# Sliding-window attention and a channel mix: the first loads ordered by hand

## The chip, the cores and the metric

The kernel runs on one core of a Trainium2 chip. The core has five engines: TensorE (PE, matrix products and transposes), VectorE (DVE), ScalarE (ACT), GpSimd (POOL) and SyncE (SP, which here only issues transfers), and 16 DMA engines that move data between the chip's memory (HBM) and the core's SBUF. Each engine works through its own instructions in order and waits on semaphores for what others make. The metric is the device time of one execution in microseconds (us); lower is better.

## What is computed

The first part is attention over 8 batches of 8 heads, with 576 positions of 64 elements. Each position sees itself and the 127 before it, and a bias falls off linearly with the distance (its slope differs from head to head). The second part mixes each position with the one before it, in two ways, and runs a gated two-layer network of width 512 to 1024 to 512.

```python
scores = scale * q @ k.T                         # B, H, S, D = 8, 8, 576, 64
bias   = -slope[h] * abs(i - j)
attn   = softmax(where(0 <= i - j < 128, scores + bias, -1e9))
x      = (attn @ v).transpose(0, 2, 1, 3).reshape(B, S, 512)
x_prev = x shifted by one position
xk     = mu_k * x + (1 - mu_k) * x_prev
xr     = mu_r * x + (1 - mu_r) * x_prev
out    = sigmoid(xr @ w_r) * (relu(xk @ w_k) ** 2 @ w_v)
```

Inputs and output are float32. The matrix products run in bfloat16.

## The kernel before

One iteration `it` of the kernel is one pair of heads `g` of one batch `b` (4 pairs, 8 batches, so 32 iterations). Its q, k and v land in a ring of four float32 slots, `ldr` for q and k and `vdr` for v. They are cast to bfloat16, q and k are transposed on PE, then come scores, exp, attention times v (AV), normalization and the transpose back:

```python
NBUF = 4
ldr = cst.tile([128, 2, NBUF, 2, NF * D], FP32, name="ldr")
vdr = cst.tile([128, NBUF, 2, NF, D], FP32, name="vdr")

def load_qk(it, npair=1, part=None): ...   # SyncE: q, k of 512 positions into slot it % 4
def load_v(it, j0=0, j1=NF): ...           # SyncE: v, one transfer for each head
def load_tail(b): ...                      # SyncE: the last 64 positions of all heads: tq (q, k), tv (v)
def cast_qk(it, part=None, fq=pool_cast, fk=vec_cast): ...   # ldr -> cs
def cast_v(it, j0=0, j1=NF): ...           # POOL: vdr -> vs_buf[it % 4]
def transp(it): ...                        # PE: cs -> tp, ACT: tp -> qk_buf[it % 4]
def scores(it, pieces, m0): ...            # PE: sa, ACT: exp -> at; DVE: times mask
def av(it, t0, t1): ...                    # PE: sa, DVE: rc, xu (normalized)
def outT(it, t0, t1): ...                  # PE: xu -> tp, ACT: xt, DVE: dl, xk, xr
```

For the first two batches (`it < NEARLY`, 8) the bias and the window are added by extra matmuls (`sid` with `dist`) instead of a mask product. Meanwhile the mask of the later batches is made (`make_mask` on ACT, `copy_mask` on DVE).

The network's work lies in a list of units, each with the PE time that it is reckoned at in ns. `run_units(n)` takes units off the list until their sum comes to n:

```python
def add_units(P, c0, c1):
    for fo in range(NFO):                                   # xk @ w_k, relu on ACT, square on DVE
        units.append(((c1 - c0) * 1.69, lambda fo=fo: mm1(P, c0, c1, fo)))
    for c in range(c0 // 128, c1 // 128):
        units.append((864, lambda c=c: mm3(P, c)))          # xr @ w_r, tanh on ACT
        units.append((864, lambda c=c: mm2(P, c0, c, 0)))   # kk @ w_v, first half
        units.append((864, lambda c=c: mm2(P, c0, c, 1)))   # second half, ot on DVE, store
```

The start: batch 0 is worked on in two ranges of positions (0 to 255, then the rest), so that PE has something to do before all of it has landed. The weights come by transfers that GpSimd issues and that cast from float32 on the way.

```python
load_qk(0, 1, 0)
load_v(0, 0, 2)
load_qk(1, 3, 0)
for g in range(1, G):
    load_v(g, 0, 2)
make_identity(nc, ident)
make_dist()
load_qk(0, 4, 1)
load_tail(0)
for g in range(G):
    load_v(g, 2, NF)
# ... first range of batch 0; at its third step (g == 2):
load_w(wk_sb, moe_w_k)
load_w(wr_sb, moe_w_r)
# ... second range of batch 0, between units of positions 0 to 255:
for g in range(-1, G + 1):
    # ... scores, casts, transposes; load_w(wv_sb, moe_w_v) at g == 0
    if 0 <= g < G:
        av(g, 2, NJ)
        load_qk(G + g)
        load_v(G + g)
        if g == 0:
            load_tail(1)
    # ...
```

In the first range all five engines follow the order of the program. From the second range on, only PE, SyncE and GpSimd do; for ACT and DVE the compiler's scheduler chooses.

From batch 1 on, one loop:

```python
for it in range(G, NIT + 2):
    b, g = divmod(it, G)
    load_qk(it + 4)
    load_v(it + 4)
    if g == 0:
        load_tail(b + 1)
    scores_full(it)
    # bud: what is left over a reserve of 5000, spread over the batch
    run_units(bud * .15)
    # ... transp_tail, units
    if it > G:
        av(it - 1, 0, NJ)
    run_units(bud * .25)
    transp(it + 2)
    cast_qk(it + 3)
    cast_v(it + 3)
    # ... cast_tail, units, masks
    if it > G:
        outT(it - 1, 0, NJ)
        # ... at g == 0: add_units of the batch that is complete
    run_units(bud * .25)
```

PSUM is shared out as two double banks for scores and AV (`p_sa`), one bank for transposes (`p_tp`) and three for the network (`p_mm`).

Of the kernel before, what the change touches and what calls it, by code (L numbers as in the profile page):

```python
# [9 lines left out]
FP32 = mybir.dt.float32  # L10
# [7 lines left out]
def kernel(  # L18
# [56 lines left out]
    xt_buf = [cst.tile([128, NPO, 2 + S], BF16, name=f"xt{i}") for i in range(2)]  # L75


    def load_tail(b):
        if b >= B:
            return  # L80
        tq = tlp.tile([128, H, D], FP32, tag="tq", name="tq")
        tv = tlp.tile([64, H, D], FP32, tag="tv", name="tv")
        T["tl", b] = (tq, tv)
        for src, dst in ((q, tq[0:64]), (k, tq[64:128]), (v, tv)):
            nc.sync.dma_start(out=dst, in_=src[b, :, SM:S, :].rearrange("h p d -> p h d"))

    def load_qk(it, npair=1, part=None):
        if not 0 <= it < NIT:
            return
        b, g = divmod(it, G)  # L90
        s0 = it % NBUF
        for i, src in enumerate((q, k)):
            hs = src[b, 2 * g:2 * g + 2 * npair]
            dst = ldr[:, i, s0:s0 + npair].rearrange("p s h c -> p (s h) c")
            if part is None:
                nc.sync.dma_start(
                    out=dst,
                    in_=hs[:, 0:SM].rearrange("h (p r) d -> p h (r d)", p=128))
            else:
                nc.sync.dma_start(  # L100
                    out=dst[:, :, 128 * part:128 * part + 128],
                    in_=hs[:, 256 * part:256 * part + 256].rearrange(
                        "h (p r) d -> p h (r d)", p=128))

    def load_v(it, j0=0, j1=NF):
        if not 0 <= it < NIT:
# [18 lines left out]
    def cast_qk(it, part=None, fq=pool_cast, fk=vec_cast):  # L125
        if not 0 <= it < NIT:
            return
        cs = csp.tile([128, 2, NF, 2, D], BF16, tag="cs", name="cs")
        T["cs", it, part] = cs
        r0, r1 = (0, NF) if part is None else (2 * part, 2 * part + 2)  # L130
        for i, f in ((0, fq), (1, fk)):
            f(cs[:, i, 0:r1 - r0].rearrange("p r h d -> p h r d"),
              ldr[:, i, it % NBUF].rearrange(
                  "p h (r d) -> p h r d", d=D)[:, :, r0:r1])
# [10 lines left out]
    def cast_tail(b):  # L145
        if b >= B:
            return
        tq, tv = T.pop(("tl", b))
        ts = csp.tile([128, H, D], BF16, tag="ts", name="ts", bufs=2)
        T["ts", b] = ts  # L150
        pool_cast(ts, tq)
        tvb = tv_buf[b % 2]
        if b < 2:
            nc.gpsimd.memset(tvb[:, :, D], 1.0)
            nc.gpsimd.memset(tvb[64:128], 0.0)
            nc.gpsimd.memset(tt_buf[b][:, :, 1], 0.0)
        pool_cast(tvb[0:64, :, 0:D], tv)


    def transp_tail(b):  # L160
        if b >= B:
            return
        ts = T.pop(("ts", b))
        tp = p_tp.tile([128, 1024], BF16, tag="tp", name="tp")
        for g in range(G):
            nc.tensor.transpose(
                tp[:, 128 * g:128 * g + 128],
                ts[:, 2 * g:2 * g + 2].rearrange("p h d -> p (h d)"), ident)
        t4 = tp[:, 0:128 * G].rearrange("p (g t c) -> p g t c", g=G, t=2)
        nc.vector.tensor_copy(out=tt_buf[b % 2][:, :, 2], in_=t4[:, :, 0])  # L170
        nc.vector.tensor_copy(out=tt_buf[b % 2][:, :, 0], in_=t4[:, :, 1])  # L171
# [30 lines left out]
    def scores(it, pieces, m0):  # L202
# [28 lines left out]
        if not early:  # L231
            nc.vector.tensor_tensor(
                out=ah, in0=ah, in1=mask[:, 2 * g:2 * g + 2, m0:m0 + w], op=ALU.mult)

    def scores_full(it):
        scores(it, ((0, 0, 256), (1, 128, 256)), 0)
        scores(it, ((2, 256, 256), (3, 384, 128), (3, 512, 64), (4, 512, 64)), 256)

    def av(it, t0, t1):
        if not 0 <= it < NIT:  # L240
# [23 lines left out]
    def outT(it, t0, t1):  # L264
# [1 line left out]
            return  # L266
        b, g = divmod(it, G)
        xu = T.pop(("xu", it, t0))
        tp = p_tp.tile([128, 1024], BF16, tag="tp", name="tp")
        for t in range(t0, t1):  # L270
            nc.tensor.transpose(  # L271
                tp[:, 128 * t:128 * t + 128],
# [39 lines left out]
    def mm3(P, c):  # L312
        xr = T["xr", P]
        pr = p_mm.tile([128, 512], FP32, tag="mm", name="pr")
        for po in range(NPO):
            nc.tensor.matmul(  # L316
                pr, lhsT=xr[:, po, 128 * c:128 * c + 128], rhs=wr_sb[:, po],
                start=(po == 0), stop=(po == NPO - 1))
        rs = otp.tile([128, DM], BF16, tag="rs", name="rs")
        T["rs", P, c] = rs  # L320
        nc.scalar.activation(out=rs, in_=pr, func=AF.Tanh, scale=0.5)  # L321

# [19 lines left out]
    ident = cst.tile([128, 128], BF16, name="ident")  # L342
    mask = cst.tile([128, H, 768], BF16, name="mask")
    dist = cst.tile([128, 768], BF16, name="dist")
    dist2 = cst.tile([128, 256], BF16, name="dist2")
    sid = cst.tile([128, H, 128], BF16, name="sid")
    MSEG = ((256, 256), (512, 192), (704, 64))
    wk_sb = cst.tile([128, NPO, DF], BF16, name="wk_sb")
# [22 lines left out]

    def make_mask(heads):
        for h in heads:
            nc.scalar.activation(out=mask[:, h, 0:256], in_=dist2,
                                 func=AF.Exp, scale=-(2.0 ** (-(h + 1))))

    def copy_mask():
        for (c0, n) in MSEG:
            nc.vector.tensor_copy(out=mask[:, 0:H, c0:c0 + n], in_=mask[:, 0:H, 0:n])

    def load_w(dst, src):
        nc.gpsimd.dma_start(out=dst, in_=src.rearrange("(i p) w -> p i w", p=128))
# [34 lines left out]
        ENG.PE, ENG.SP, ENG.Pool, ENG.Activation, ENG.DVE})  # L417
    order.__enter__()
    load_qk(0, 1, 0)
    load_v(0, 0, 2)  # L420
    load_qk(1, 3, 0)
    for g in range(1, G):
        load_v(g, 0, 2)
    make_identity(nc, ident)
    make_dist()
    load_qk(0, 4, 1)
    load_tail(0)
    for g in range(G):
        load_v(g, 2, NF)


    make_sid(0)
    make_sid(1)
    cast_qk(0, 0, act_cast, vec_cast)
    transp_part(0, 0)
    cast_qk(1, 0, act_cast, vec_cast)
    cast_v(0, 0, 2)
    load_mu()
    for g in range(G + 2):
        if g < G:  # L440
            scores(g, ((0, 0, 256), (1, 128, 128)), 0)
        if g + 1 < G:
            transp_part(g + 1, 0)
            make_sid(2 * g + 2)
            make_sid(2 * g + 3)
            cast_v(g + 1, 0, 2)
        if g + 2 < G:
            cast_qk(g + 2, 0, act_cast, vec_cast)
        if g == 2:
            load_w(wk_sb, moe_w_k)  # L450
            load_w(wr_sb, moe_w_r)
        if 0 <= g - 1 < G:
            av(g - 1, 0, 2)
        if g == 4:
            cast_qk(0, 1, act_cast, vec_cast)
            transp_part(0, 1)
        if 0 <= g - 2 < G:
            outT(g - 2, 0, 2)
    order.__exit__(None, None, None)
    order = tc.manual_schedule(engines={ENG.PE, ENG.SP, ENG.Pool})  # L460
    order.__enter__()
    add_units(0, 0, 256)

    def second(g, which):
        if not 0 <= g < G:
            return
        if which == 0:
            scores(g, ((1, 256, 128), (2, 256, 256)), 128)
        else:
            scores(g, ((3, 384, 128), (3, 512, 64), (4, 512, 64)), 512)  # L470

    for g in range(-1, G + 1):
        bud = left() / max(1, G - g)
        second(g + 1, 0)
        if g == -1:
            cast_tail(0)
            transp_tail(0)
        run_units(bud * .2)
        second(g + 1, 1)
        if g + 2 < G:  # L480
            cast_qk(g + 2, 1, act_cast, vec_cast)
            transp_part(g + 2, 1)
        if g + 1 < G:
            cast_v(g + 1, 2, NF)
        if g == 0:
            load_w(wv_sb, moe_w_v)
        run_units(bud * .3)
        if 0 <= g < G:
            av(g, 2, NJ)
            load_qk(G + g)  # L490
            load_v(G + g)
            if g == 0:
                load_tail(1)
        run_units(bud * .3)
        if g >= 1:
            outT(g - 1, 2, NJ)
        if g == 2:
            cast_qk(G)
            transp(G)
            cast_v(G)  # L500
        if g == 3:
            cast_tail(1)
            cast_qk(G + 1)
            cast_v(G + 1)
        run_units(bud * .2)
    transp(G + 1)
    transp_tail(1)
    cast_qk(G + 2)
    cast_v(G + 2)
    add_units(0, 256, 512)  # L510

    for it in range(G, NIT + 2):
        b, g = divmod(it, G)
        load_qk(it + 4)
        load_v(it + 4)
        if g == 0:
            load_tail(b + 1)
        scores_full(it)
        if it >= NIT:
            bud = left() if it == NIT else 1 << 30  # L520
        elif g == 0:
            bud = min(left(), 5500.0)
        else:
            bud = max(left() - RESERVE, 0) / (G - g)
# [1 line left out]
        if g == 2:  # L526
            transp_tail(b + 1)
        run_units(bud * .1)
        if it > G:
            av(it - 1, 0, NJ)  # L530
        run_units(bud * .25)
        transp(it + 2)
        cast_qk(it + 3)
        cast_v(it + 3)
        if g == 1:
            cast_tail(b + 1)
        run_units(bud * .25)
        if it == G:
            pool_cast(dist2, dist[:, 0:256])
        if it < NEARLY:  # L540
            make_mask(range(2 * g, 2 * g + 2))
        if it == NEARLY - 1:
            copy_mask()
        if it > G:
            outT(it - 1, 0, NJ)
            if g == 0:
                P, e = divmod(b - 1, 2)
# [4 lines left out]
                    add_units(P, 0, 512)  # L552
        run_units(bud * .25)
    order.__exit__(None, None, None)


# [1 line left out]
_INS = ['q', 'k', 'v', 'moe_mu_k', 'moe_mu_r', 'moe_w_k', 'moe_w_v', 'moe_w_r']  # L558
# [26 lines left out]
```

## Time and profile before

| | |
|---|---|
| median of 3 runs | 291.3 us (288.97 to 294.21) |
| span of the profiled execution | 290.8 us |
| instructions | 6032 |
| read from HBM, written to it | 33.56 MB, 9.44 MB |
| transfers on SyncE's queue, on GpSimd's | 48.4% and 5.6% of 16 engines' span |
| largest groups | pv matmuls (kk with w_v) 73.6 us, kk product on DVE 37.6 us |

How to read it: a row of 40 digits shows how busy an engine was in each fortieth of the span (7.3 us each), 9 for 90% or more. "PEclk" is the clock that was granted to PE, in tenths of its full speed. The chain is followed back from the last instruction: each piece is what the next one waited for. In a list of waits the engine on the left sat idle until the one on the right was done; DMA on the right means a load had not landed. A group is named by the tile that it writes and those that it reads: `ldr<-in_k_dram` is a load of k into the ring, `cs<-ldr` the cast out of it, `tq` and `tv` are the tails. PE's busy time is modelled (matmuls overlap), so it says when PE had work and not how near it was to its peak.

### The profile page before, as it was taken

What the parts mean: (1) busy time and instruction counts of PE and PEld (TensorE: products, weight loads), DVE (VectorE), ACT (ScalarE), POOL (GpSimd) and SP (SyncE); (2) the same over time, 40 slices, a digit from 0 to 9 for tenths busy, and PEclk for the clock granted to TensorE, in tenths of its full rate; (3) what the DMA queues carried; (4) which work ended last, traced back from release to release, by engine and by line L of the source; (5) the groups of instructions that cost most, each with busy time, mean ns of one, the idle gap of its engine ahead of it and who ended that gap; (6) DMA issues with size and microseconds to landing.
All of it is one profiled execution on the core that took longest, in us unless ns stands there. A gap on an engine that the chain in (4) does not pass through costs nothing.

```text
span 290.8 us, 6032 instructions
## 1 busy us (share of the span) xinstructions
PE 248.3 (85%) x2304; PEld 144.1 (50%) x2304; DVE 207.1 (71%) x434; ACT 182.1 (63%) x297; POOL 68.7 (24%) x111
## 2 busy tenths in 40 slices
PE   2859648796769899979999999889899999998994
PEld 1326414454436466545565575545464755544461
DVE  1472315757688898897899797997697978875341
ACT  4654613597758667767676686866695858725350
POOL 5516051405124312421132122321042120000000
PEclk9999977999999999999999999999999999999999
DMA  6997994999109057671564482914851511011021
GB/s 177 230 201 178 180 159 136 275 243 263 28 36 253 17 172 194 202 197 39 163 198 131 159 214 88 291 31 133 245 150 70 149 37 39 0 74 72 36 74 72
DMA packets 73389, 40.77 MB, mean 140 GB/s; under 512 B 48272, under 2 KB 68240, under 8 KB 73360
## 3 DMA queue, kind: packets, MB, share of 16 engines
q1 hardware_dynamic: 71200, 37.76, 48.4%
q0 software_dynamic: 2160, 2.63, 5.6%
q8 instruction: 18, 0.29, 0.4%
q14 instruction: 11, 0.09, 0.1%
HBM read 33.56 MB, written 9.44 MB: 148 GB/s over the span
## 4 chain that ended last, share of the span: by engine, by line
PE 48%; DVE 20%; ACT 15%; DMA 10%; issue 4%; SPq 2%; POOL 0%; DVEq 0%; ACTq 0%; POOLq 0%
PE pv L330 13%; PE pr L316 8%; DMA ldr<-in_k_dram 7%; PE sa L250 4%; DMA tq<-in_k_dram 4%; PE tp L271 4%; DVE kk L307 3%; DVE xk L289 3%; PE tp L179 3%; DVE xu L260 2%; PE sa L227 2%; ACT rs L321 2%; DVE xr L289 2%; DVE ot L336 2%; ACT rl L305 2%
## 5 line engine op out<-in xcount | busy, mean ns | idle before, releaser
L330 PE MATMUL pv<-wv_sb,kk 128*128 128x512 bf16 x288 | 73.6, 386 | 2.7 <-DMA wv_sb<-in_moe_w_v_dram 2.7
L301 PEld LDWEIGHTS <-wk_sb 128*128 128x128 bf16 x416 | 38.9, 100 | 21.3 <-issue 3.9
L307 DVE TENSOR_TENSOR kk<-rl 128x256 bf16<-128x256 bf16 (+2 forms) x104 | 37.6, 381 | 9.5 <-ACT rl L305 8.3
L321 ACT ACTIVATE rs<-pr 128x512 bf16<-128x512 f32 x36 | 21.7, 602 | 27.9 <-PE pr L316 27.8
L330 PEld LDWEIGHTS <-kk 128*128 128x128 bf16 x288 | 25.7, 98 | 27.0 <-issue 3.8
L316 PE MATMUL pr<-wr_sb,xr 128*128 128x512 bf16 x144 | 37.6, 385 | 0.0
L336 DVE SCALAR_TENSOR_TENSOR ot<-rs,pv 128x512 f32<-128x512 bf16 x36 | 24.5, 680 | 10.3 <-PE pv L330 10.3
L120 DVE CAST cs<-ldr 128x512 bf16<-128x512 f32 (+1 forms) x36 | 15.2, 422 | 22.5 <-DMA ldr<-in_k_dram 19.1
L260 DVE TENSOR_TENSOR xu<-sa,rc 128x640 bf16<-128x640 f32 (+2 forms) x36 | 27.0, 749 | 1.1
L271 PE MATMUL tp<-ident,xu 128*128 128x128 bf16 x160 | 15.5, 224 | 12.0 <-DVE xu L260 4.5
L116 POOL TENSOR_SCALAR cs<-ldr 128x512 bf16<-128x512 f32 x28 | 21.4, 766 | 14.0 <-DMA ldr<-in_q_dram 10.4
L271 PEld LDWEIGHTS <-xu 128*128 128x128 bf16 x160 | 11.5, 99 | 22.3 <-DVE xu L260 12.3
L179 PE MATMUL tp<-ident,cs 128*128 128x128 bf16 x224 | 17.1, 219 | 5.3 <-DVE tt_102 L171 2.6
L179 PEld LDWEIGHTS <-cs 128*128 128x128 bf16 x224 | 14.4, 98 | 10.7 <-DVE tt_102 L171 3.4
L230 ACT ACTIVATE at_99<-sa 128x1024 bf16<-128x1024 f32 (+2 forms) x17 | 15.8, 971 | 6.1 <-PE sa L227 6.1
L316 PEld LDWEIGHTS <-xr 128*128 128x128 bf16 x144 | 13.1, 99 | 12.3 <-issue 0.6
L287 DVE TENSOR_TENSOR dl<-xt_106 128x576 bf16<-128x576 bf16 (+2 forms) x20 | 8.8, 442 | 13.1 <-ACT xt_106 L278 13.1
L230 ACT ACTIVATE at_101<-sa 128x1024 bf16<-128x1024 f32 (+2 forms) x17 | 15.8, 974 | 3.5 <-PE sa L227 3.4
L116 POOL TENSOR_SCALAR vs_94<-vdr 128x512 bf16<-128x512 f32 (+1 forms) x9 | 6.4, 708 | 48.0 <-PE sa L250 35.8
L230 ACT ACTIVATE at_98<-sa 128x1024 bf16<-128x1024 f32 (+2 forms) x17 | 15.9, 972 | 2.2 <-PE sa L227 2.2
L287 DVE TENSOR_TENSOR dl<-xt_107 128x576 bf16<-128x576 bf16 x16 | 7.3, 458 | 13.2 <-ACT xt_107 L278 13.2
L278 ACT COPY xt_106<-tp 128x576 bf16<-128x576 bf16 (+2 forms) x20 | 10.9, 546 | 9.0 <-PE tp L271 9.0
(316 smaller groups left out, 481.1 us busy)
## 6 DMA issues: line engine op xcount, KB each, us to landing
out_dram<-ot SPq DMA_DIRECT2D x36, 256.0 KB, 2.1
ldr<-in_q_dram SPq DMA_DIRECT2D x28, 256.0 KB, 4.0
ldr<-in_k_dram SPq DMA_DIRECT2D x28, 256.0 KB, 4.2
vdr<-in_v_dram SPq DMA_DIRECT2D x56, 128.0 KB, 4.4
vdr<-in_v_dram SPq DMA_DIRECT2D x16, 64.0 KB, 4.2
tq<-in_q_dram SPq DMA_DIRECT2D x8, 128.0 KB, 5.3
tq<-in_k_dram SPq DMA_DIRECT2D x8, 128.0 KB, 4.6
wk_sb<-in_moe_w_k_dram POOLq DMA_DIRECT2D x1, 1024.0 KB, 9.8
```

Source lines behind the costliest of these rows:

```text
L116: nc.gpsimd.tensor_scalar(out=dst, in0=src, scalar1=1.0, scalar2=0.0, op0=ALU.mult, op1=ALU.add)
L179: nc.tensor.transpose(tp[:, 128 * n:128 * n + 128], cs[:, n // NF, n % NF].rearrange("p h d -> p (h d)"), ident)
L230: nc.scalar.activation(out=ah, in_=sa[:, :, 0:w], func=AF.Exp, scale=float(scale))
L260: nc.vector.tensor_tensor(out=xu[:, t0:t1].rearrange("p t h d -> p h t d"), in0=a5[:, :, :, 0:D], in1=rc[:, :, 0:nt, None].to_broadcast([1 ...
L271: nc.tensor.transpose(tp[:, 128 * t:128 * t + 128], xu[:, t].rearrange("p h d -> p (h d)"), ident)
L287: nc.vector.tensor_tensor(out=dl[:, 0:c1 - c0], in0=xc, in1=xp, op=ALU.subtract)
L301: nc.tensor.matmul(ps[:, 0:n], lhsT=wk_sb[:, po, 128 * fo:128 * fo + 128], rhs=xk[:, po, c0:c1], start=(po == 0), stop=(po == NPO - 1))
L307: nc.vector.tensor_tensor(out=kk[:, fo, 0:n], in0=rl[:, 0:n], in1=rl[:, 0:n], op=ALU.mult)
L316: nc.tensor.matmul(pr, lhsT=xr[:, po, 128 * c:128 * c + 128], rhs=wr_sb[:, po], start=(po == 0), stop=(po == NPO - 1))
L321: nc.scalar.activation(out=rs, in_=pr, func=AF.Tanh, scale=0.5)
L330: nc.tensor.matmul(pv, lhsT=kk[:, fo, o:o + 128], rhs=wv_sb[:, fo], start=(fo == 0), stop=(fo == NFO - 1))
L336: nc.vector.scalar_tensor_tensor(out=ot, in0=T.pop(("rs", P, c)), scalar=1.0, in1=pv, op0=ALU.add, op1=ALU.mult)
```

## The change

Its purpose is that what is needed first also lands first. Batch 0 is loaded in the order of its use: v in blocks of 128 positions for all heads, the tails of q and k ahead of the second range, the tail of v last. The weights follow. Batch 1's loads are held back behind w_r by a tiny copy on GpSimd that writes into `ldr` and reads `wr_sb`. Every later load is issued right after the casts that free its slot, by `feed`.

Around this the program up to the end of batch 1 is laid out anew. Batch 0's two ranges are one run of eight equal steps without units. Then come units of positions 0 to 511 (now with one mask on ACT for each of the last eight mm1), and batch 1 with the rest of them. All five engines follow the order of the program until batch 1 is through.

```diff
+    def load_v_block(b, j):
+        s0 = (b * G) % NBUF
+        nc.sync.dma_start(
+            out=vdr[:, s0:s0 + G, :, j].rearrange("p s h d -> p (s h) d"),
+            in_=v[b, :, 128 * j:128 * j + 128, :].rearrange("h p d -> p h d"))
...
     load_qk(0, 1, 0)
-    load_v(0, 0, 2)
+    load_v_block(0, 0)
     load_qk(1, 3, 0)
-    for g in range(1, G):
-        load_v(g, 0, 2)
+    load_v_block(0, 1)
+    load_tail(0, (0, 1))
+    load_qk(0, 4, 1)
+    load_v_block(0, 2)
+    load_v_block(0, 3)
+    load_tail(0, (2,))
     make_identity(nc, ident)
     make_dist()
-    load_qk(0, 4, 1)
-    load_tail(0)
-    for g in range(G):
-        load_v(g, 2, NF)
...
+    def cast(i):
+        if i < 2 * G:
+            cast_qk(i % G, i // G, act_cast if i < G else pool_cast, vec_cast)
...
+    for i in range(2 * G):
+        score(i)
+        if i == G - 1:
+            transp_tail(0)
+        trans(i + 1)
+        if i + 1 < G:
+            make_sid(2 * i + 2)
+            make_sid(2 * i + 3)
+        castv(i + 1)
+        if i == G - 2:
+            cast_tail(0)
             load_w(wk_sb, moe_w_k)
+        cast(i + 2)
+        if i == G:
+            pool_cast(tv_buf[0][0:64, :, 0:D], T["tl", 0][1])
+        if i == G:
             load_w(wr_sb, moe_w_r)
+            load_w(wv_sb, moe_w_v)
+        if i >= 1:
+            av(*span(i - 1))
+        if i >= 2:
+            outT(*span(i - 2))
+    av(*span(2 * G - 1))
+    outT(*span(2 * G - 2))
+
+    nc.gpsimd.tensor_copy(out=ldr[:, :, 0, 0, 0:1], in_=wr_sb[:, 0:2, 0:1])
+    load_qk(G)
+    load_tail(1, (0, 1))
+    load_v(G)
+    load_tail(1, (2,))
+    for g in range(1, G):
+        load_qk(G + g)
+        load_v(G + g)
...
+    def feed(it, fk=vec_cast):
+        cast_qk(it, None, pool_cast, fk)
+        cast_v(it)
+        load_qk(it + 4)
+        load_v(it + 4)
+        if it % G == 0:
+            load_tail(it // G + 1)
...                      (units: 16 mm1 of 256 columns, 4 mm3, 8 halves of mm2)
+    run_units(1800)
+    outT(*span(2 * G - 1))
+    run_units(4500)
+    run_units(1800)
+    feed(G, pool_cast)
+    cast_tail(1)
+    run_units(1800)
+    transp(G)
+    feed(G + 1, pool_cast)
+    transp_tail(1)
+    run_units(1000)
+    for it in range(G, 2 * G):
+        g = it - G
+        scores(it, *HALF0)
+        transp(it + 1)
+        if it > G + 1:
+            outT(it - 2, 0, NJ)
+        scores(it, *HALF1)
+        bud = max(left() - 3500, 0) / (2 * G - it)
+        run_units(bud * .5)
+        if g < len(MSEG):
+            copy_mask(g)
+        if it > G:
+            av(it - 1, 0, NJ)
+        feed(it + 2, pool_cast)
+        run_units(bud * .5)
+    outT(2 * G - 2, 0, NJ)
     order.__exit__(None, None, None)
     order = tc.manual_schedule(engines={ENG.PE, ENG.SP, ENG.Pool})
...                      (bridge: AV and transposes of the last pair, three times run_units(1000))
-    for it in range(G, NIT + 2):
+    for it in range(2 * G, NIT + 2):
         b, g = divmod(it, G)
-        load_qk(it + 4)
-        load_v(it + 4)
-        if g == 0:
-            load_tail(b + 1)
         scores_full(it)
...
         transp(it + 2)
-        cast_qk(it + 3)
-        cast_v(it + 3)
+        feed(it + 3)
```

Buffers change with it: `cs` from 3 to 4, `rs` from 3 to 6; the transposes of `outT` in batches 0 and 1, and those of the tails always, now go to a bank of `p_mm` instead of the single one of `p_tp`. A copy of `dist` for the masks (`dist2`) is gone.

## The prediction

> **What bounds the kernel now.** I read the page first, busy times and the 40 slices, to see whether one engine is full everywhere.
>
> ```profile
> PE 248.3 (85%) x2304; PEld 144.1 (50%) x2304; DVE 207.1 (71%) x434; ACT 182.1 (63%) x297; POOL 68.7 (24%) x111
> PE   2859648796769899979999999889899999998994
> PEclk9999977999999999999999999999999999999999
> DMA  6997994999109057671564482914851511011021
> ```
>
> PE is at 9 or 8 in nearly every slice from the 14th on, and ragged in the first thirteen, where the DMA row is at its fullest. So there are two regimes. I cut the span into stages with the table by stretches (columns: length, busy time and count of PE, weight load, DVE, ACT, POOL, then clock, DMA share, GB/s). The cuts are batch 1's first scores at 55.2, batch 2's start, about 80, and the period of two batches after that.
>
> ```profile
> 0.00:4.00 4.00, 0.52 (x5) 0.42 (x6) 0.93 (x6) 1.69 (x2) 1.88 (x10) 1.00 0.37 100
> 4.00:16.00 12.00, 8.52 (x65) 3.87 (x63) 4.61 (x20) 6.98 (x14) 5.65 (x16) 1.00 1.14 238
> 16.00:30.00 14.00, 11.15 (x92) 6.87 (x90) 5.63 (x18) 6.64 (x15) 5.56 (x11) 1.00 0.97 186
> 30.00:55.20 25.20, 15.51 (x131) 8.25 (x129) 12.28 (x31) 10.19 (x19) 6.85 (x12) 0.86 0.86 180
> 55.20:80.00 24.80, 19.85 (x245) 12.69 (x243) 15.59 (x38) 20.10 (x34) 7.09 (x12) 1.00 0.79 187
> ...
> 110.90:171.20 60.30, 56.37 (x559) 33.31 (x558) 53.04 (x102) 42.77 (x66) 15.10 (x20) 1.00 0.56 157
> 171.20:231.70 60.50, 56.43 (x559) 33.36 (x558) 52.31 (x102) 42.76 (x66) 16.38 (x20) 1.00 0.55 153
> ```
>
> Two batches take 60.3 and 60.5 us with PE busy 56.4: the steady part is bound by PE and repeats. Between 30 and 55.2 PE is busy 15.5 of 25.2 us, at a clock of 0.86. The chain of waits (start, length, what) says why:
>
> ```profile
> 3.26 4.65 DMA ldr<-in_k_dram
> ...
> 9.83 10.76 DMA tq<-in_k_dram
> ...
> 26.14 3.85 DMA ldr<-in_k_dram
> ...
> 36.19 6.06 DMA ldr<-in_k_dram
> ```
>
> Four loads, 25.3 us, set the first 42 us. The list of waits for 0 to 80 us agrees (us in total, times, longest):
>
> ```profile
> DVE cs L120 <- DMA ldr<-in_k_dram: 19.1, 3, 8.6
> POOL vs_94 L116 <- DMA vdr<-in_v_dram: 12.2, 2, 9.5
> PE pv L330 <- DMA wv_sb<-in_moe_w_v_dram: 2.7, 1, 2.7
> ```
>
> The timeline of SyncE adds two dates: batch 1's first k load is issued at 26.14 and its second only at 36.19, behind three tail loads. The timeline of PE has scores of iterations 4, 5, 6, 7, 8 start at 55.3, 63.1, 67.7, 73.1 and 77.8.
>
> **What the Trainium skill says.** "DMA: Bandwidth & Descriptors", section "Issuing engines are not separate DMA queues": transfers from different engines run on the same 16 DMA engines and interleave. The trace agrees: the 1 MB wk landed 9.8 us after issue while the tails and v of batch 0 were in flight, and those came late too (tq 10.8 us). So the order in which transfers are handed out decides what comes first. Same page, "Specifications": runs under 512 B don't reach line rate. Here 48272 of 73389 packets are under 512 B (v and the tails move 256 B runs), and the stretch 4 to 16 us shows share 1.14 at only 238 GB/s, so I take the measured rates. "TensorE: Matmul & The Clock Gate", "What's actually happening": an idle PE gets a lower clock. The trace agrees: PEclk 7 in two slices just around the waits, and a 512 wide pv matmul at 631 ns at 44 us against a mean of 386.
>
> **The change part by part.** Everything up to the start of iteration 8 (batch 2) is rewritten; after it the loop is the old one but for the place of the loads. So the sum is: when does iteration 8 start, how much PE work is then left over from before it, and does the steady rate move.
>
> (1) Loads of batch 0. Bytes are unchanged: q, k, v are 8 x 576 x 64 x 4 B x 3 = 3.54 MB per batch; weights are 2.6 MB as written. The old order put qk and v of range 0, then qk of range 1, tails, v. The new one puts v as blocks of all heads, tails of q and k before qk of range 1, and tail v last. The qk of range 1 now has 2.8 MB before its end instead of 2.56, at the 220 GB/s of that stage 1.1 us later (its first cast was at 15.5, so about 17). wk is issued after the tail cast, about 13 us against 10.6. With 3.54 + 1.05 MB at 0.2 to 0.22 MB per us everything of batch 0 and wk is in at about 23 to 24.
>
> (2) Attention of batch 0 as eight equal steps. The first four ran at 3.9, 8.5, 10.8, 13.5 and stay, at about 2.5 us each. In the second range a step costs, by the groups kept apart by shape, ACT 0.81 + 0.60 (exp) + 0.58 (qk copy) + 0.43 (xt copy) = 2.4 us and DVE 0.29 + 0.19 + 0.56 + 0.33 + 2 x 0.55 = 2.5 us. In strict order I choose 3 us. Step 4 starts at 17.5, but the AV of step 4 needs tail v, at about 23. Then steps 6 and 7 at 25 and 28, and the last AV at about 31.
>
> (3) MoE of tokens 0 to 512. The units are 16 x 432 + 4 x 864 + 8 x 864 ns = 17.3 us of PE, and these costs are real: eight pv matmuls take 1.73 us in the chain. Of these 10.9 us come before the loop over batch 1. ACT has to do 16 relu x 0.38 + 4 tanh x 0.60 + 8 masks x 0.41 = 11.8 us there, a little more than PE. With the transposes of iteration 4 in between: 31 + 12 + 1 = 44 us for the first scores of batch 1, against 55.3.
>
> (4) Weights wr, wv and batch 1. wr and wv are issued at step 4 once tail v is cast, about 24. The tiny copy on POOL makes batch 1's loads wait for wr, about 29.5 (24, + 0.8 for the issue, + 2.1 which is what the smallest load of the page takes to land, + 0.52 MB at 0.2, 2.6). Then 1.05 + 3.54 MB at 0.2 take 23 us, so iteration 4's data are in at 36 to 39, iteration 7's at 50 to 52. They are needed at 42 and at about 50: just in time, perhaps 1 us late.
>
> (5) Iterations 4 to 7. The old ones took 4.9 us each from 63.1 to 77.8. The new ones have DVE 0.21 + 0.82 + 0.46 + 2 x 0.82 = 3.1, plus mask copies of up to 0.7 and one ot of 0.68, and PE about 3.4 of attention plus 0.7 of units. I keep 4.9: 44 + 19.6 = 63.6.
>
> (6) Bridge to iteration 8: the AV and transposes of iteration 7, tail, transposes of 9, and 3 us of units, together about 5 us: 68.5. At that point the old kernel had 5.0 us of units (its reserve) and AV and output transposes of 7 (1.1 us) still to do, the new one 3.5 - 3.0 = 0.5 us. That is 5.6 us less to do.
>
> Gain: (77.8 - 68.5) + 5.6 = 14.9 us.
>
> (7) Loads at their casts in the steady loop. An iteration takes 7.5 us (60.3 / 8), a 256 KB load lands in about 4. The loads were issued one iteration ahead of their cast; they now go almost four ahead. But PE is 93% busy there, so this hides only what was hidden: I count 0.
>
> Sum: 291.3 - 14.9 = 276.4 us; I say 276.5.
>
> **The rivals.** (a) The first stage is bound by bytes, and a new order only moves the wait. For: DMA share near 1 until 42 us, but for 25 to 30. Against: batches 0 and 1 with weights are 9.7 MB, some 49 us at 0.2, while the old kernel reached iteration 8 only at 77.8; between 42 and 50 us it moved just 99 GB/s. If the chaining behind wr leaves the queue empty for 4 us more and iteration 5 waits, the gain falls to 8 or 9 us: 283. (b) The hand order of ACT and DVE becomes the bound: until now only the very first part was ordered by hand on them, now all of batches 0 and 1 is. One late operand holds up all behind it. For: ACT was busy 20.1 of 24.8 us in the stretch 55.2 to 80. If each of twelve steps costs 1 us more, the gain is 3 us: 288. (c) POOL becomes slow. It takes over both casts in range 1 and in batch 1; "SBUF — State Buffer", section "Who interferes with whom", says that GpSimd and a DVE instruction in a two-port mode shut each other out. The trace has POOL casts of one shape from 0.62 to 0.97 us. POOL is 24% busy, so I give it under 2 us. (d) Stores wait in SyncE's queue behind loads that wait for casts. The casts of v wait for AV up to 7.6 us in the old kernel; but PE puts that AV before the units whose stores follow. Up to 3 us in all. (e) Better: the idle 3.5 us of PE between 80 and 110.9 and all of the early gap go: 268.
>
> **Range and chances.** The three estimates that carry the sum are the end of batch 0's attention (31, give or take 3), the start of batch 1 (44, give or take 4) and the step of 4.9 us (0.7 times four). Together about 6 us each way; rivals b and d make the upper side longer. Range 267 to 286. Faster by over 2% means below 285.5; only rival b or several together prevent that: 0.86. Within 2%: 0.09. Slower by over 2%: 0.05.
>
> **What would show it.** In the new profile: scores of iteration 4 at about 44 and of 8 at about 68.5; no wait of DVE or POOL on a load above 4 us after 24; PE clock without the 7s; two batches still 60 us in the steady part; the pieces of the chain up to 40 us ACT and DVE where they were DMA. Wrong would be: iteration 8 near 75 with ACT waiting for PE and DVE in turn (rival b), a hole in DMA traffic between 24 and 32 (rival a), or a period above 61 us with waits of ot behind stores (rival d).

## The result and the profile after

The changed kernel takes 279.4 us (median of 4 runs, 278.03 to 280.6) against 291.65 us before (median of 4 runs, the 3 ahead of the prediction and one more): the ratio is 0.961, with a 95% interval of 0.951 to 0.970. The prediction was 276.5 us with a range of 267 to 286.

The first lines of the page of the changed kernel, the same rows as those shown of before:

```profile
PE 242.4 (88%) x2271; PEld 142.2 (52%) x2304; DVE 206.6 (75%) x428; ACT 181.0 (66%) x293; POOL 71.0 (26%) x121
PE   2866899968988989989999898899999999899994
PEclk9996899988999999999999999999999999999999
DMA  7996999999783737926596349607502120022122
```

PE is at 8 or 9 from the fifth slice on but for a 6 in the ninth, instead of from the fourteenth. The clock still has dips, a 6 and an 8 in the fourth and fifth slices and 8s in the ninth and tenth. The stages, cut anew at the first scores of batch 1 (45.3) and at iteration 8 (70.4), in the table by stretches:

```profile
16.00:30.00 14.00, 10.66 (x124) 6.03 (x122) 9.22 (x28) 8.65 (x16) 5.65 (x11) 0.76 0.86 150
30.00:45.30 15.30, 13.71 (x114) 9.50 (x114) 11.60 (x32) 11.58 (x32) 6.10 (x11) 1.00 1.20 248
45.30:57.00 11.70, 10.61 (x126) 5.71 (x126) 3.61 (x7) 9.07 (x11) 8.48 (x15) 1.00 1.10 256
57.00:70.40 13.40, 10.07 (x105) 5.97 (x104) 11.29 (x23) 5.88 (x7) 4.57 (x7) 0.87 1.04 265
...
101.00:161.30 60.30, 55.76 (x549) 33.12 (x555) 53.52 (x104) 42.91 (x65) 15.65 (x21) 1.00 0.59 158
161.30:221.70 60.40, 56.48 (x554) 33.90 (x562) 53.08 (x102) 42.92 (x65) 15.81 (x21) 1.00 0.39 112
```

Two batches of the steady part take 60.3 and 60.4 us, as before. The second row is what the change is about: 30 to 45 us is now 90% busy for PE with units of batch 0, while DMA brings batch 1 at 248 GB/s. In the old kernel PE was 62% busy from 30 to 55. The two stretches ahead of iteration 8 are not good: DVE has 3.61 us of work in 11.7 and then 11.29 in 13.4.

One cut organizes all that follows. I read three dates from the timeline of PE: the start of batch 1's first scores, the start of iteration 8's scores, and from there to the end of the span. The dates are of one profiled execution of each kernel; each ratio is of several executions, beside the kernel before on the same chip (medians 291.65 to 292.83), with slow ones left out.

| kernel | batch 1 starts | iteration 8 starts | rest of the span | time, ratio to before (95%) |
|---|---|---|---|---|
| before | 55.3 | 77.8 | 213.0 | 1 |
| changed | 45.3 | 70.4 | 205.8 | 0.961 (0.951 to 0.970) |
| changed, once more (a0) | 47.6 | 71.4 | 205.8 | 0.956 (0.949 to 0.964) |
| e1, steady loads late | 47.2 | 70.5 | 205.2 | 0.952 (0.945 to 0.958) |
| e2, old order of batch 0 | 48.6 | 73.4 | 206.0 | 0.964 (0.958 to 0.970) |
| e3, no hold | 45.1 | 75.8 | 205.7 | 0.964 (0.957 to 0.971) |
| e4, ACT and DVE scheduled | 41.0 | 66.7 | 205.8 | 0.945 (0.936 to 0.953) |
| f1, outT behind AV | 46.9 | 70.8 | 205.8 | 0.955 (0.948 to 0.961) |
| f2, tail of v early | 44.1 | 69.1 | 205.8 | 0.947 (0.941 to 0.954) |
| f3, f1 and f2 | 45.4 | 68.6 | 205.8 | 0.944 (0.938 to 0.950) |
| f4, f3 and e4 | 42.2 | 66.0 | 205.8 | 0.932 (0.924 to 0.940) |
| b1, before with batch 1's loads early | 54.1 | 76.2 | 213.5 | 1.002 (0.998 to 1.006) |
| b2, before with the new order of batch 0 | 51.6 | 74.0 | 212.7 | 0.987 (0.979 to 0.994) |
| b3, before with two k casts moved | 49.4 | 73.1 | 213.6 | 0.989 (0.980 to 0.997) |

The rest of the span is nearly the same within each family: 212.7 to 213.6 and 205.2 to 206.0. Nothing that was done to the loads or orders moved it by more than 0.9 us; the step between the families is the units and AV of batches 0 and 1 that the old program still had to do after iteration 8's scores, and some idle time. The trace of the changed kernel lacks 27 matmuls there, so I take e2's, which has them all: PE's busy time from iteration 8 on is 189.9 us (1773 matmuls) against 194.8 before (1813), 4.9 of the 7.0 to 7.2 us, and the other 2.1 to 2.3 us are idle time of PE. All the rest of the gain lies before iteration 8.

### The profile page after: what moved, and what is told of

It is laid out like the page before. It is cut to its first block, busy times and chain, and to the rows that moved or that the text cites. A ratio compares the mean times of both kernels' runs of the same rounds, so it can differ in the third digit from the quotient of the medians.

```text
span 276.2 us, 6003 instructions
## 1 busy us (share of the span) xinstructions
PE 242.4 (88%) x2271; PEld 142.2 (52%) x2304; DVE 206.6 (75%) x428; ACT 181.0 (66%) x293; POOL 71.0 (26%) x121
## 4 chain that ended last, share of the span: by engine, by line
PE 45%; DVE 21%; ACT 10%; DMA 8%; issue 7%; SPq 4%; POOL 4%; POOLq 0%; DVEq 0%; ACTq 0%
PE pv L347 14%; PE pr L333 7%; DVE xu L274 4%; DVE xk L306 4%; PE sa L264 3%; PE tp L288 3%; DMA vdr<-in_v_dram 3%; DMA ldr<-in_k_dram 3%; DVE kk L324 2%; DMA tq<-in_k_dram 2%; DVE xr L306 2%; PE sa L238 2%; ACT rs L338 2%; ACT at_99 L241 2%; DVE ot L353 2%
## 5 line engine op out<-in xcount | busy, mean ns | idle before, releaser
L347 PE MATMUL pv<-wv_sb,kk 128*128 128x512 bf16 x274 | 70.2, 382 | 1.2 <-issue 0.7
L318 PEld LDWEIGHTS <-wk_sb 128*128 128x128 bf16 x416 | 38.3, 98 | 21.7 <-issue 4.9
L353 DVE SCALAR_TENSOR_TENSOR ot<-rs,pv 128x512 f32<-128x512 bf16 x36 | 24.4, 679 | 15.7 <-PE pv L347 15.7
L333 PE MATMUL pr<-wr_sb,xr 128*128 128x512 bf16 x131 | 35.5, 379 | 0.6
L126 POOL TENSOR_SCALAR cs<-ldr 128x512 bf16<-128x512 f32 (+1 forms) x38 | 28.0, 740 | 8.3 <-DMA ldr<-in_q_dram 7.3
L288 PEld LDWEIGHTS <-xu 128*128 128x128 bf16 x160 | 10.4, 99 | 21.7 <-DVE xu L274 18.4
L241 ACT ACTIVATE at_99<-sa 128x1024 bf16<-128x1024 f32 (+2 forms) x17 | 16.0, 976 | 5.8 <-PE sa L238 5.8
L333 PEld LDWEIGHTS <-xr 128*128 128x128 bf16 x144 | 13.1, 98 | 12.0 <-issue 0.2
L130 DVE CAST cs<-ldr 128x512 bf16<-128x512 f32 (+1 forms) x30 | 14.2, 473 | 6.5 <-DMA ldr<-in_k_dram 6.4
L288 PE MATMUL tp<-ident,xu 128*128 128x128 bf16 x120 | 10.7, 220 | 9.3 <-DVE xu L274 7.4
L241 ACT ACTIVATE at_101<-sa 128x1024 bf16<-128x1024 f32 (+2 forms) x17 | 15.9, 973 | 3.0 <-PE sa L238 3.0
L241 ACT ACTIVATE at_98<-sa 128x1024 bf16<-128x1024 f32 (+2 forms) x17 | 15.9, 973 | 2.9 <-PE sa L238 2.9
L241 ACT ACTIVATE at_100<-sa 128x1024 bf16<-128x1024 f32 (+2 forms) x17 | 15.9, 975 | 2.3 <-PE sa L238 2.3
L190 PE MATMUL tp<-ident,cs 128*128 128x128 bf16 x224 | 17.1, 219 | 0.0
L304 DVE TENSOR_TENSOR dl<-xt_106 128x576 bf16<-128x576 bf16 (+2 forms) x20 | 8.0, 398 | 9.1 <-ACT xt_106 L295 9.1
```

The source lines that it names most:

```text
L126: nc.gpsimd.tensor_scalar(out=dst, in0=src, scalar1=1.0, scalar2=0.0, op0=ALU.mult, op1=ALU.add)
L190: nc.tensor.transpose(tp[:, 128 * n:128 * n + 128], cs[:, n // NF, n % NF].rearrange("p h d -> p (h d)"), ident)
L241: nc.scalar.activation(out=ah, in_=sa[:, :, 0:w], func=AF.Exp, scale=float(scale))
L288: nc.tensor.transpose(tp[:, 128 * t:128 * t + 128], xu[:, t].rearrange("p h d -> p (h d)"), ident)
L318: nc.tensor.matmul(ps[:, 0:n], lhsT=wk_sb[:, po, 128 * fo:128 * fo + 128], rhs=xk[:, po, c0:c1], start=(po == 0), stop=(po == NPO - 1))
L333: nc.tensor.matmul(pr, lhsT=xr[:, po, 128 * c:128 * c + 128], rhs=wr_sb[:, po], start=(po == 0), stop=(po == NPO - 1))
```

## The experiments

**e1: the loads of the steady loop back at the loop's head.**

```diff
+        if it + 4 >= 3 * G:
+            load_qk(it + 4)
+            load_v(it + 4)
+            ...                       # and the tail; feed() no longer issues these
         scores_full(it)
```

> The changed kernel with one part undone: from batch 3's data on, each load is issued at the head of the loop, one iteration ahead of its cast, as in the kernel before. Theory (the steady part is bound by PE and hid its loads already): same time as the changed kernel, 278 to 281 us, and two batches in the steady part still take 60.3 us. Rival (the deeper prefetch pays in the steady part): 283 us or more, with a longer period.

Measured: 277.9 us, 0.952 (0.945 to 0.958); the rest of the span is 205.2 us. The theory stands: the last part of the change, a load with every cast, gains nothing that can be measured in the steady loop. The interval lies across that of the changed kernel, and the rest of the span did not grow.

**e2: the old order of batch 0's loads.**

```diff
-    load_v_block(0, 0)
+    load_v(0, 0, 2)
     load_qk(1, 3, 0)
     ...                               # v by heads, tails behind q and k, second half of v last
```

> The changed kernel with the old order of batch 0's loads (v by heads, tails behind q and k of the second range, the second half of v last). Theory (the order of batch 0's loads is worth little, because the program behind it waits for the last of 3.5 MB either way): within 2 us of the changed kernel, 278 to 282. Rival (the order is what the change lives from): 285 us or more.

Measured: 281.2 us, 0.964 (0.958 to 0.970). The median is 2.5 us above that of a0 (278.7) and 1.8 above the first one. So it is little, as the theory had it, and the rival is out. The intervals overlap, so the size alone rests on the medians; iteration 8 starts 2 to 3 us later than in the two traces of the changed kernel.

**b2: the new order of batch 0's loads in the kernel before, and nothing else.**

> The kernel before with the new order of batch 0's loads alone (v in blocks, tails of q and k ahead of the second range, tail of v last). Theory (the order within batch 0 is worth little by itself): 289 to 293 us. Rival (tails that land 5 us earlier free GpSimd, and with it wv and the second range): 284 to 288 us.

Measured: 288.8 us, 0.987 (0.979 to 0.994), 3.6 us less than before. I expected next to none, the rival expected more; it lies between the two. With e2 it gives the same picture from both sides: the order within batch 0 is worth 2 to 4 us.

**b1: batch 1's loads early, in the kernel before.**

```diff
             cast_v(g + 1, 2, NF)
+            load_qk(G + g + 1)
+            load_v(G + g + 1)
+            if g == -1:
+                load_tail(1)
...
             av(g, 2, NJ)
-            load_qk(G + g)
-            load_v(G + g)
-            if g == 0:
-                load_tail(1)
```

> The kernel before with one part of the change alone: batch 1's loads stand right behind the casts that free their slots, and so ahead of the first stores in SyncE's queue. Theory (the old kernel lost its time because batch 1's loads stood in SyncE's queue behind a store that waited for a result, from 38.8 to 46.7 us, while DMA moved 99 GB/s): batch 1's data land by about 46 us instead of 58, and half or more of the gain comes, 281 to 286 us. Rival (the bytes of weights and batch 1 are the bound, and earlier issue only makes them share): the weights come later by as much, 288 to 293 us.

Measured: 293.3 us, 1.002 (0.998 to 1.006). My theory falls. The loads did go earlier: the last q and k of batch 1 are issued at 39.7 and 40.3 instead of 49.3 and 50.3. But batch 1's first scores start at 54.1 instead of 55.3. The rival's form of it isn't right either: the weights didn't come later (PE's first product with wv starts at 36.7 instead of 38.2). The trace of DVE shows what held. First the kernel before (start, length, engine, line, operation; in brackets the idle time ahead of it and its releaser), then b1:

```profile
42.27 0.62 DVE L120 CAST cs<-ldr 128x512 bf16<-128x512 f32 x1 [8.64 <-DMA ldr<-in_k_dram]
42.81 0.18 DVE L259 RECIPROCAL rc<-sa 128x6 f32<-128x6 f32 x1
43.02 0.56 DVE L260 TENSOR_TENSOR xu<-sa,rc 128x384 bf16<-128x384 f32 x1
```

```profile
39.89 0.88 DVE L120 CAST cs<-ldr 128x512 bf16<-128x512 f32 x1 [7.33 <-DMA ldr<-in_k_dram]
40.69 0.18 DVE L259 RECIPROCAL rc<-sa 128x6 f32<-128x6 f32 x1
40.91 0.56 DVE L260 TENSOR_TENSOR xu<-sa,rc 128x384 bf16<-128x384 f32 x1
```

The first line of each is a cast of batch 1's k (512 columns). The two behind it normalize batch 0 (6 columns of sums, 384 of output: the second range). DVE works in order, so batch 0's normalization waits for batch 1's load, and PE waits for that:

```profile
40.92 0.34 PE L227 MATMUL sa<-qk_93 64*128 64x128 bf16 x4
43.64 0.39 PE L216 MATMUL sa<-dist,sid 128*128 128x256 bf16 x2 [2.38 <-DVE xu L260]
```

In b1 the same matmul of `dist` waits 3.03 us for xu. The load that "set" the chain was not needed by the work that it held up. The scheduler had put its cast in front.

b1 is no clean test of an earlier load, though. The load that counted was issued 5.6 us earlier (30.6 against 36.2) but landed only 2.4 us earlier (39.9 against 42.3), 9.2 us after its issue instead of 6.1, while more transfers were under way. That agrees with the rival's sharing, only on batch 1's own data, and the block stayed. So b1 leaves open whether the block or the date of the load is the cost; b3 tells them apart.

**b3: those casts taken off DVE, in the kernel before.**

```diff
-            cast_qk(G)
+            cast_qk(G, None, pool_cast, pool_cast)
...
-            cast_qk(G + 1)
+            cast_qk(G + 1, None, pool_cast, pool_cast)
```

> The kernel before with the casts of k of iterations 4 and 5 on GpSimd instead of DVE, and nothing else. Theory (in the old kernel batch 1's k casts stand on DVE ahead of batch 0's normalization, so DVE, idle 6.2 us until 30.1 and 8.6 us until 42.3, holds back batch 0 until batch 1's loads land; this, and not the landing alone, is what PE loses its time to): 3 to 6 us less than before, 286 to 289 us, no DVE wait on a k load above 2 us after 24 us. Rival (PE in that stretch waits for wv and the batch 1 data themselves): 290 to 293 us.

Measured: 289.45 us, 0.989 (0.980 to 0.997), 3.4 us less than before by the medians, as much as the theory expected, though the time lies just above its 286 to 289; batch 1's first scores come 5.9 us earlier in the trace. Of these, 2.2 us come from wv, for which PE waits in both and which landed sooner here (36.0 against 38.2) though it was issued at the same time; from PE's first product with wv to batch 1 it takes 13.4 us, against 17.1 in the kernel before and 17.4 in b1. The casts run on GpSimd, and DVE in the same stretch is this:

```profile
33.28 0.20 DVE L259 RECIPROCAL rc<-sa 128x6 f32<-128x6 f32 x1 [2.00 <-PE sa L250]
33.51 0.56 DVE L260 TENSOR_TENSOR xu<-sa,rc 128x384 bf16<-128x384 f32 x1
37.68 0.33 DVE L287 TENSOR_TENSOR dl<-xt 128x320 bf16<-128x320 bf16 x1 [3.61 <-ACT xt L278]
```

No wait for a load is left in this stretch, though no load was moved; the normalization that began at 42.8 in the kernel before begins at 33.3. What PE still loses there is the wait for wv, 2.75 us at 36, with the first half of mm2 standing in PE's order ahead of batch 0's work: the same kind of block, on another engine (moving it was not tried).

**e3: no hold of batch 1's loads behind w_r.**

```diff
-    nc.gpsimd.tensor_copy(out=ldr[:, :, 0, 0, 0:1], in_=wr_sb[:, 0:2, 0:1])
```

> The changed kernel without the tiny copy on GpSimd that holds batch 1's loads back behind w_r. Theory (the hold keeps the weights from sharing the DMA engines with batch 1, and PE needs the weights first): batch 1's loads are issued from about 17 us on instead of 28.5, wr and wv land 3 to 6 us later, the first units wait, and the time is 0 to 4 us longer, 279 to 283. Rival (the hold leaves the DMA engines idle for nothing, the stretch 16 to 30 us moves only 150 GB/s): batch 1 starts at the same time or earlier and the time falls to 275 to 278.

Measured: 280.8 us, 0.964 (0.957 to 0.971), 2.1 us above a0 by the medians, within what the theory expected, but the intervals overlap. Half of the theory is seen: wr landed 7.0 us after its issue instead of 5.3 and wv 13.6 instead of 11.3, so they were there at 30.6 and 38.0 instead of 28.2 and 35.1. But PE first needs them at 36.1 and 44.2 and waits for neither: the units began at 30.3 and batch 1 at 45.1, no later than in the changed kernel. The time goes afterwards, between 52 and 57:

```profile
51.46 2.39 DVE L395 COPY mask<-mask 128x1536 bf16<-128x1536 bf16 x1
53.76 0.20 DVE L273 RECIPROCAL rc<-sa 128x10 f32<-128x10 f32 x1
55.23 0.43 DVE L130 CAST cs<-ldr 128x512 bf16<-128x512 f32 x1 [1.26 <-POOL cs L126]
55.57 0.81 DVE L274 TENSOR_TENSOR xu<-sa,rc 128x640 bf16<-128x640 f32 x1
```

The mask copy takes 2.39 us here and 0.56 in the changed kernel. Behind it a cast of batch 2's k waits for GpSimd, and it stands ahead of an xu for which PE waits 3.3 us. In the changed kernel the same cast stands behind that xu (58.88 and 59.62): without the hold the scheduler orders the two the other way round. So in that trace the hold brought the weights 2 to 3 us sooner, which nothing waited for; taking it out brought back the block of the kernel before. The profiled execution is the slowest of its four (283.3), so how much of this the others have is open.

**e4: ACT and DVE left to the scheduler from the first units on.**

```diff
+    order.__exit__(None, None, None)
+    order = tc.manual_schedule(engines={ENG.PE, ENG.SP, ENG.Pool})
+    order.__enter__()
     run_units(1800)
     outT(*span(2 * G - 1))
```

> The changed kernel with the program order on ACT and DVE ended before the first units, so that in batch 1 only PE, SyncE and GpSimd follow the program, as in the kernel before. Theory (the order by hand on ACT and DVE is not what gains; the earlier data are): 277 to 282 us. Rival 1 (the hand order gains): 284 us or more. Rival 2 (the hand order costs, since PE waits 2 us at 59.8 for an xu that stands on DVE behind older work): 275 to 277 us.

Measured: 275.6 us, 0.945 (0.936 to 0.953). Rival 2 has the size, though the runs scatter (274.2 to 279.9) and the interval just meets that of the changed kernel. Its reason is not what the trace shows: in batch 1 PE still waits for xu, 1.10 us at 54.6 and 3.12 at 60.5, more than the 1.95 and 1.00 of the changed kernel. The gain lies ahead of batch 1, which starts at 41.0 instead of 45.3, and it has two parts.

In the order of instructions on DVE the copies of the mask now stand among batch 0's steps, and ACT is busy 10.6 us of the first 16 instead of 8.8: the scheduler moved the masks into time in which both engines waited for loads. In the changed kernel they lie in the units and in batch 1. From the first units to batch 1 it takes 12.7 us instead of 14.3, so this part is 1.6 us. The other 2.7 us lie ahead of the first units (28.3 instead of 31.0), where GpSimd casts the tail of v. The changed kernel, then e4:

```profile
22.38 0.61 POOL L126 TENSOR_SCALAR tv_104<-tv 64x512 bf16<-64x512 f32 x1 [3.48 <-DMA tv<-in_v_dram]
```

```profile
19.67 0.78 POOL L126 TENSOR_SCALAR tv<-tv 64x512 bf16<-64x512 f32 x1
```

The loads up to there are the same, but in this execution the tail landed 5.5 us after its issue instead of 9.6, so PE did not wait for it. Whether the new order brought that or chance did isn't shown; it is the wait that f2, below, takes away. The granted clock differs too, 1.00 from 16 to 30 us against 0.76.

**a0, f1, f2, f3: the changed kernel beside two repairs.** f1 moves the output transposes and the mask copy behind AV in batch 1's loop, f2 loads the tail of v with the tails of q and k:

```diff
         transp(it + 1)
-        if it > G + 1:
-            outT(it - 2, 0, NJ)
         scores(it, *HALF1)
...
             av(it - 1, 0, NJ)
+        if it > G + 1:
+            outT(it - 2, 0, NJ)
+        if g < len(MSEG):
+            copy_mask(g)                # was ahead of av
```

```diff
-    load_tail(0, (0, 1))
+    load_tail(0)
...
     load_v_block(0, 3)
-    load_tail(0, (2,))
```

> The changed kernel once more, beside its variants on the same chip: 278 to 281 us.

> The changed kernel; in the loop over batch 1 the output transposes and the mask copy stand behind AV, so that on DVE the xu of the newer iteration goes ahead of dl, xk, xr of the older one. Theory (PE's wait of 1.95 us at 59.8 for xu, and the cold clock after it, are a cost of the strict order on DVE): 2 to 3 us less than the changed kernel, about 276 to 277, and scores of iteration 8 at 68. Rival (the wait is slack that the reserve of units takes up later): the same as the changed kernel within 1 us.

> The changed kernel with the tail of v loaded together with the tails of q and k. Theory (GpSimd stands still from 18.9 to 22.3 us for the tail of v, and the issue of wr and wv stands behind it, and with that batch 1's loads): wr and wv issued at about 19.5 to 20.5, batch 1's loads at about 25 to 26, and 2 to 3 us less, about 276 to 277. Rival (the bytes are the bound: v lands later by what the tail takes): within 1 us of the changed kernel.

> The changed kernel with both: tail of v early, and output transposes behind AV in batch 1. Theory (the two costs lie one after the other and add): 4 to 6 us less than the changed kernel, 273 to 276. Rival: no more than the better of the two alone.

Measured: a0 278.7 us; f1 278.3; f2 276.05; f3 274.75. What f1 was to repair is seen on DVE in the changed kernel:

```profile
51.12 0.69 DVE L353 SCALAR_TENSOR_TENSOR ot<-rs,pv 128x512 f32<-128x512 bf16 x1 [5.97 <-PE pv L347]
51.72 0.56 DVE L395 COPY mask<-mask 128x1536 bf16<-128x1536 bf16 x1
52.19 0.21 DVE L273 RECIPROCAL rc<-sa 128x10 f32<-128x10 f32 x1
52.44 0.82 DVE L274 TENSOR_TENSOR xu<-sa,rc 128x640 bf16<-128x640 f32 x1
55.47 0.46 DVE L304 TENSOR_TENSOR dl<-xt_107 128x576 bf16<-128x576 bf16 x1 [2.21 <-POOL tv_104 L126]
55.97 1.04 DVE L306 SCALAR_TENSOR_TENSOR xk<-dl,muk_sb,xt_107 128x576 bf16<-128x576 bf16 x1
56.93 1.16 DVE L306 SCALAR_TENSOR_TENSOR xr<-dl,mur_sb,xt_107 128x576 bf16<-128x576 bf16 x1
58.01 0.71 DVE L395 COPY mask<-mask 128x512 bf16<-128x512 bf16 x1
58.65 0.20 DVE L273 RECIPROCAL rc<-sa 128x10 f32<-128x10 f32 x1
58.88 0.82 DVE L274 TENSOR_TENSOR xu<-sa,rc 128x640 bf16<-128x640 f32 x1
```

DVE has nothing to do for 6 us, then the older iteration's dl, xk, xr and a mask copy stand ahead of the newer one's xu (58.88), and PE waits 1.95 us for it. (The releaser of dl is put down to a cast of tv that it does not read; the copy of xt on ACT ends at 55.37, just ahead.) With f1 that wait goes, and the trace has another of the same 1.95 us at 63.9: the wait moved. f1 alone gains nothing that can be measured, as its rival says.

f2 gains 2.7 us by the medians, as its theory has it; its four runs (274.8 to 276.8) all lie below those of a0 (277.9 to 279.4). The queue of GpSimd shows it, first a0, then f2:

```profile
24.23 0.61 POOL L126 TENSOR_SCALAR tv<-tv 64x512 bf16<-64x512 f32 x1 [5.18 <-DMA tv<-in_v_dram]
24.80 0.80 POOL L398 DMA_DIRECT2D wr_sb<-in_moe_w_r_dram  x1
25.59 0.89 POOL L398 DMA_DIRECT2D wv_sb<-in_moe_w_v_dram  x1
...
30.45 0.23 POOL L502 CAST ldr<-wr_sb 128x2 f32<-128x2 bf16 x1 [2.50 <-DMA wr_sb<-in_moe_w_r_dram]
```

```profile
19.74 0.78 POOL L126 TENSOR_SCALAR tv<-tv 64x512 bf16<-64x512 f32 x1
20.47 0.80 POOL L398 DMA_DIRECT2D wr_sb<-in_moe_w_r_dram  x1
21.27 0.89 POOL L398 DMA_DIRECT2D wv_sb<-in_moe_w_v_dram  x1
...
27.08 0.19 POOL L501 CAST ldr<-wr_sb 128x2 f32<-128x2 bf16 x1 [3.46 <-DMA wr_sb<-in_moe_w_r_dram]
```

GpSimd no longer stands still before the tail's cast, wr goes out 4.3 us sooner and batch 1's loads follow 3.4 us sooner than in a0; against the other trace of the changed kernel (22.9 and 28.3) it is 2.5 and 1.2 us, so part of this is how an execution starts. f3 is 4.0 us below a0, at the lower edge of what was expected of both; it is only 1.3 below f2, and their runs overlap, so that f1 adds something to f2 isn't shown.

**f4: f1, f2 and e4 in one kernel.**

> The changed kernel with the tail of v early, the output transposes behind AV in batch 1, and ACT and DVE left to the scheduler from the first units on. Theory (the early tail and the free order each take away a different wait): 272 to 275 us, below each of the two alone. Rival (both shorten the same stretch before the first units): the same as the better one alone, 275 to 277.

Measured: 273.2 us (272.94 to 273.57), ratio 0.932 (0.924 to 0.940). It is the fastest kernel of the study, 6.8% below the kernel before; by intervals it lies below the changed kernel (0.949 to 0.964 beside its repairs), and it touches those of f3 and e4. That is the theory's 272 to 275. Iteration 8 starts at 66.0. Beside f2, which has the tail of v early as well, the first units begin at 29.8 in both, and batch 1 starts at 42.2 instead of 44.1: 1.9 us for the free order alone (f1 acts only after that date), close to the 1.6 us of e4. PE's waits for xu are not all gone (2.17 us at 58.9).

## Why the prediction was right, and where it was not

The time, 279.4, lies in the range, 2.9 us above the 276.5. The gain was forecast too large, and the sum came as near as it did partly by luck, because errors of opposite sign met. Step by step, on the profiled execution (276.2 us of span against 290.8, so 14.6 us less):

- Step 1, batch 0's loads: q and k of the second range were cast at 14.8, not 17; the weight wk was issued at 13.4 (13), tail v was cast at 22.4 (23). Right, the first even too late by 2.2, and the value of this order by itself, 2 to 4 us, agrees from both sides (e2, b2).
- Step 2: the last AV of batch 0 at 30.3 (31). Right.
- Step 3: batch 1's first scores at 45.3 (44). The size is off by 1.3, in a0 (47.6) by 3.6.
- Step 4: batch 1's loads issued at 28.5 (29.5), and the cast of iteration 7's v began at 48.5 (data at 50 to 52). Right.
- Step 5: from the first scores of iteration 4 to the AV of iteration 7 (63.9) it is 18.6 us, 4.65 for each iteration (4.9). Nearly right as a number, but its reason (so much work for each engine) isn't what sets it: the first scores follow each other after 2.2, 4.5 and 4.4 us, and the order on DVE makes PE wait, as the lines above show.
- Step 6, the bridge: 6.5 us to the scores of iteration 8 (5), which start at 70.4 (68.5). From there PE has 4.9 us less to do (5.6), and 2.3 us less of idle time, which the prediction did not reckon with. A start 1.9 us late and a rest 1.6 us shorter than forecast all but cancel: 7.4 + 7.2 = 14.6 against 14.9. In a0 it is 6.4 + 7.2 = 13.6.
- Step 7, steady loads: 0 was counted, and e1 found none. Right.

The profiled pair flatters the forecast: the medians differ by 12.3 us, and that of a0 by 13.1 from the kernel before beside it. The forecast of 276.5 is a ratio of 0.949 to the 291.3 of then, at the lower end of the intervals or below (0.951 and, for a0, 0.949).

Of rival a, the hole in the traffic is there in part: from 20 to 30 us DMA moves 126 GB/s at a share of 0.76. But PE waits for no load of batch 1, so it costs nothing that the trace shows. Rival b, the order by hand on ACT and DVE, was rated as a risk of 1 us for each of twelve steps. It is real but smaller: e4 takes back about 3 us, and of that only 1.6 to 1.9 us are shown to be the order's. Rival d found no support (two batches take 60.3 and 60.4 us); c is seen in single instructions only (xk 1.04 and xr 1.16 us beside casts of GpSimd, against 0.82). The sign "PE clock without the 7s" failed: 16 to 30 us runs at 0.76. So did the sign of no wait above 4 us on a load after 24 us: GpSimd waits 6.9 us for q until 35.3, and that costs nothing, because PE has units until 42. The chain up to 40 us was to be ACT and DVE; it still holds two loads, 6.98 us for k of batch 0 and 7.85 us for v of batch 1, instead of four with 25.3 us.

What was wrong is the reading of the kernel before. I wrote that four loads set the first 42 us, from the chain. The chain names the load that released DVE; it does not say that the work behind on DVE needed it. b3 moves no load and gains 3.4 us, so a cast of another batch at the head of DVE's order was one part. b1 issued that load sooner and gained nothing, but it landed little sooner, so b1 alone proves neither reading. The changed kernel has no cast of batch 1 ahead of batch 0's last normalization. That it gains the rest through its layout (batch 0 in eight steps without units, units when the weights are there, batch 1 after that) follows by subtraction only: if the 3.6 us of b2 and the 3.4 of b3 add up, which was not run, some 5 of the 12.3 us are left for it, and the layout was not run without the rest.

## What to carry to other kernels

When a chain ends in a load, look at what stands behind the instruction that waits for it on the same engine: if that belongs to other data, try moving the waiting instruction and not only the load: here two casts moved gained 3.4 us, and loads issued earlier gained nothing, since the one that counted landed hardly sooner. Keep prefetch casts of the next batch behind the current batch's work on each in-order engine, and let nothing that starts other transfers stand behind a wait on the same queue (here wr and wv stood behind a cast that waited up to 5.2 us, and loading its data sooner gained 2.7). A reserve of work left over, and the date at which a steady loop begins, add up to the whole difference between two kernels with the same loop: cut there first.

## What was not expected of the hardware

The start of the program varies from execution to execution though its instructions are the same: tail v was cast at 22.4 in one trace of the changed kernel and at 24.2 in the other, and the first units began at 31.0 and 33.1. With the same loads it was cast at 24.4 in e1, 24.0 in f1 and 19.7 in e4. A DVE copy of 128 x 1536 took 0.56 us in the changed kernel, where GpSimd stood idle for most of it, and 2.39 in e3, where GpSimd's casts ran beside it; the Trainium skill, "SBUF — State Buffer", section "Who interferes with whom", says that such a copy and a GpSimd instruction can shut each other out, and the number agrees with that, but no run isolated it. PE's granted clock fell to 0.76 from 16 to 30 us in the changed kernel and in f4, and stayed at 1.00 in e4, which has the same loads and the same order on PE up to there; what sets it off is open.
